# Silu in one activation, merged exponentials, and weight sums read back from DRAM, in a fused attention and gated-MLP kernel

## The chip, the cores and the metric

One core of a Trainium2 chip. The metric is the device time of the kernel in microseconds, the median of several runs; one further execution was profiled.

## What is computed

A windowed attention (window 32 in plain heads, 32 steps of 4 tokens in dilated heads), whose output feeds a gated MLP:

```python
scores = np.where(masks, q @ k.T / sqrt(64), -1e9)      # 8 batches, 8 heads, 576 tokens, head size 64
attn = exp(scores - max); attn = attn / (sum(attn) + 1e-9)
x = (attn @ v) as [4608 tokens, 512]
g = x @ w_gate                                          # 512 -> 1536
silu = g * (1.0 / (1.0 + np.exp(-g)))
return (silu * (x @ w_val)) @ w_out                     # 1536 -> 512
```

## The kernel before

The 4608 tokens are worked in six chunks. All MLP products run as float32r matmuls on operands that are split in a high and a low part, three products for each exact one.

The first three chunks have 512 tokens each. Each has 12 steps of 128 hidden features (`for s in range(NS)`). A step is 12 gate matmuls into `bank_g`, 12 value matmuls into `bank_v` (both L587) and the 12 output matmuls of the step before into `bank_o` (L636). ScalarE takes tanh(g/2) from `bank_g` (`act_tanh`, L608), DVE makes (tanh + 1) * g from it and the bank (`dve_u`, L613), then times 0.5 and the value bank (`dve_h`, L618); ScalarE and POOL split the result in two parts (`h_hi` L623, `h_lo` L628).

The last three chunks (`for ci in range(NC)`) have 1024 tokens each and multiply in blocks: sums of quarter matrices go through seven products instead of eight. A chunk has a gate stage, 6 pairs of features x 7 products x 2 matrices of 6 matmuls each (`gate_val`, L934), and an output stage of 7 x 6 x 2 groups of 3 matmuls (`outs`, L934). `keep` (L939) copies the two first banks out on ScalarE after some products, `total` adds a bank and a kept copy on DVE (L895), and `gated` makes the hidden value: tanh on ScalarE (L960), two instructions on DVE (L962, L963).

During the first chunk the weights arrive as 64-bit floats, in 24 half rows, and are turned to float32 pairs in five steps: `w_exp` (a Prelu on ScalarE), `w_shift`, `w_bits` (DVE, L280 or L283), `w_split_hi` (ScalarE), `w_split_lo` (POOL, L294). `w_load` (L243) asks for the next half row on SP's queue when a raw buffer is free.

During the second and third chunk `mix_stage` prepares the sums of weights that the seven products need, 18 steps of three stages: `mix_parts` (DVE, L801) adds the high and low parts of the kept weights, `mix_sums` (DVE L807 to L812, ScalarE L810 and L814) makes the sums, `mix_low` (DVE, L823) their low parts; `plain_parts` (L779) and `mix_out` (L831) store them to DRAM on SP's queue. POOL's queue reads them back in the last chunks (`ask`).

The attention runs in 36 packs beside all this. A pack is visited twice: an "A" visit does the scores on TensorE, `norm` of the pack before and `shift` on DVE, the exponentials on ScalarE (`far_exps`, L492 and L487) and four small exchanges of the two results on SP's queue (L497); a "B" visit the transposes. The packs 4 to 35 go through `far_exps`, 4 to 8 of them in the first chunk; none falls into the last chunk. Slots for the visits are written out in `visits`; the order on each engine is the framework's, with `behind` and `issue_after` as constraints.

Of the kernel before, what the change touches and what calls it, by code (L numbers as in the profile page):

```python
# [10 lines left out]
F32 = mybir.dt.float32  # L11
# [5 lines left out]
ALU = mybir.AluOpType  # L17

P = 128
# [21 lines left out]

NPLAIN = 3
CS = 512
NT = 7
# [2 lines left out]
KEPT = {0: 0, 2: 1, 4: 0}  # L49
SUMS = {1: ((0, 0), 1, 0), 4: ((1, 1), 2, 0), 5: ((1, 0), 1, 0), 6: ((0, 1), 2, 1)}  # L50

SEQ = [(0, 2, 1, 3, 4, 5, 6)] + [tuple(range(NT))] * (NP - 1)
PIECE = 1024
NPG = NT * NP
# [87 lines left out]
def attention_moe(ctx, tc, qkb, vb, w, masks, ident, out):  # L142
# [24 lines left out]


    pieces = tc.dram_tile([NPIECE, P, PIECE], F32, name="pieces")

    def at(o, n, dt=F32):

# [103 lines left out]
    def w_bits(u, a=0, b=3):  # L276
        y = wst[u]["y"][:, a:b]
        lo, hi = [x[:, a:b] for x in w_parts(u)]
        if by_act(u):
            nc.vector.scalar_tensor_tensor(out=y, in0=hi, scalar=3, in1=lo,  # L280
                                           op0=ALU.logical_shift_left, op1=ALU.bitwise_or)
        else:
            nc.vector.scalar_tensor_tensor(out=y, in0=lo, scalar=29, in1=y,  # L283
                                           op0=ALU.logical_shift_right, op1=ALU.bitwise_or)

    def w_place(u):
        return [wt[u][:, a:a + WU].rearrange("p (a b) -> p a b", a=3) for a in (0, WU)]

# [29 lines left out]
    def w_one(c):  # L318
        u = done[c]
        done[c] += 1  # L320
        if c == "E":
            w_exp(u)
        elif c == "T":
            w_shift(u)
        elif c == "B":
            w_bits(u)
            while ready["w"] and w_load():
                pass
        elif c == "H":
            w_split_hi(u)  # L330
        else:
            w_split_lo(u)
# [9 lines left out]
    FN = FQN  # L342
    o = M_ATT
    early, later = {}, {}
    for k, n in (("qk", QKB), ("v", NG * NH * (D + 1)), ("e", TP), ("pt", TP)):
        later[k] = Ring(n, o)
        o += n
    later["y"] = Ring(TP, M_CONST)
# [95 lines left out]
    def scores(m, two, masked):  # L444
# [9 lines left out]
        for j in range(NH):  # L454
            for g in range(NG):
                q, k = BQ * (NH * g + j), FQN + pk(m).kcol[g, j] + o
                for h in range(2):
# [2 lines left out]
                                     lhsT=t[r, q:q + BQ], rhs=t[r, k:k + w], start=not masked,  # L460
                                     stop=not masked or j == NH - 1, skip_group_check=True)

    def shift(m, two, pool, masked):

        mx, s, e = pool["bm"](2 * NH), pool["pt"](TP), pool["e"](TP)
        w = BK - 1 + masked
        a = 512 - BK - w * (NH - 1)
        x = two[:, :, a:]
        x = bass.AP(x.tensor, x.offset, [*x.ap[:2], [w, NH], [1, BK]])
        sx, ex = [t.rearrange("q (h j k) -> q h j k", h=2, j=NH) for t in (s, e)]  # L470
        if masked:
            nc.vector.tensor_copy(out=sx, in_=x)
        else:
            n, o = pk(m).far
            f = far_sb[:, BK * n:BK * n + BK]
            f = bass.AP(f.tensor, f.offset, [f.ap[0], [BK * (o - n), 2], [0, NH], [1, BK]])
            nc.vector.tensor_tensor(out=sx, in0=x, in1=f, op=ALU.add)
        n = 2 * NH
        nc.vector.reduce_max(out=mx, in_=s.rearrange("q (x k) -> q x k", x=n), axis=mybir.AxisListType.X)
        last["s"] = nc.vector.tensor_tensor(out=e.rearrange("q (c x k) -> q c x k", c=2, x=n),  # L480
                                            in0=s.rearrange("q (x c k) -> q c x k", x=n, c=2),
                                            in1=mx.unsqueeze(1).unsqueeze(3).broadcast_to([P, 2, n, BQ]), op=ALU.subtract)
        st[m]["e"], st[m]["s"] = e, s

    def exps(m):
        e = st[m]["e"]
        last["e"] = nc.scalar.activation(out=e, in_=e, func=AF.Exp, scale=0.125)  # L487

    def far_exps(m):

        e, s = st[m]["e"], st[m]["s"]
        nc.scalar.activation(out=s, in_=e, func=AF.Exp, scale=0.125)  # L492
        exps(m)
        for g in range(0, NG, 2):
            for to in range(2):
                by = 1 - to
                nc.sync.dma_start(out=e[BQ * (g + to):BQ * (g + to) + BQ, TP // 2 * by:TP // 2 * by + TP // 2],  # L497
                                  in_=s[BQ * (g + by):BQ * (g + by) + BQ, TP // 2 * to:TP // 2 * to + TP // 2])
# [104 lines left out]
    t_ring = Ring(CH, M_H, M_H + CH)  # L603
    hh_ring = Ring(CH, M_H + 2 * CH)

    def act_tanh(i):
        t = t_ring()
        last["t"] = nc.scalar.activation(out=t, in_=bank_g[:, :CH], func=AF.Tanh, scale=0.5)  # L608
        hst[i] = [t, None, None]

    def dve_u(i):
        t = hst[i][0]
        last["h"] = nc.vector.scalar_tensor_tensor(out=t, in0=t, scalar=1.0, in1=bank_g[:, :CH],  # L613
                                                   op0=ALU.add, op1=ALU.mult)

    def dve_h(i):
        t = hst[i][0]
        last["h"] = nc.vector.scalar_tensor_tensor(out=t, in0=t, scalar=0.5, in1=bank_v[:, :CH],  # L618
                                                   op0=ALU.mult, op1=ALU.mult)

    def h_hi(i):
# [169 lines left out]
    def mix_parts(n):  # L791
        i, which = divmod(n, 3)
        q = q_at.rearrange("p (f h c) -> p f h c", f=2, h=2)
        for f in range(2):
# [3 lines left out]
            for v, third in ([(u, slice(0, 3, 2))], [(u, slice(1, 2)), (u + 1, slice(0, 1))], [(u + 1, slice(1, 3))])[which]:  # L798
# [2 lines left out]
                nc.vector.tensor_tensor(out=q[:, f, h:h + k], in0=hi, in1=lo, op=ALU.add)  # L801
                h += k

    def mix_sums(n):

        a11, a12, a21, a22 = halves(n)
        nc.vector.tensor_tensor(out=a22, in0=a21, in1=a22, op=ALU.add)  # L807
        nc.vector.tensor_tensor(out=a21, in0=a11, in1=a21, op=ALU.subtract)
        with behind("e"):
            nc.scalar.copy(out=row(l_at[:, :, 0], n, 1), in_=row(q_at.rearrange("p (n c) -> p n c", n=4), n, 1))  # L810
        nc.vector.tensor_tensor(out=a11, in0=a22, in1=a11, op=ALU.subtract)
        nc.vector.tensor_tensor(out=a12, in0=a12, in1=a11, op=ALU.subtract)  # L812
        with behind("e"):
            nc.scalar.copy(out=row(l_at[:, :, 0], n, 0), in_=row(q_at.rearrange("p (n c) -> p n c", n=4), n, 0))  # L814
# [21 lines left out]
    def mix_stage():  # L836
        nonlocal mixed
        n, stage = divmod(mixed, 3)
        mixed += 1
        if n < 3 * NP:  # L840

            with behind("h", "x", "s"):
                (mix_parts, mix_sums, mix_low)[stage](n)
            with tc.issue_after(last["w"].ins):
                if stage == 0:
                    plain_parts(*divmod(n, 3))
                elif stage == 2:
                    mix_out(n)


# [103 lines left out]
    def gated(i, t):  # L954
        if t not in SUMS:
            return
        a, b = SUMS[t][0]
        g = total(t, 0, g_ring)
        f = f_ring()
        nc.scalar.activation(out=f, in_=g, func=AF.Tanh, scale=0.5)  # L960
        v = total(t, 1, v_ring)
        nc.vector.scalar_tensor_tensor(out=f, in0=f, scalar=1.0, in1=g, op0=ALU.add, op1=ALU.mult)  # L962
        nc.vector.scalar_tensor_tensor(out=hq[a, b, i], in0=f, scalar=0.5, in1=v, op0=ALU.mult, op1=ALU.mult)  # L963
        if t == 6:
            tt(nc.gpsimd, h1[i], hq[0, 1, i], hq[0, 0, i])
            tt(nc.gpsimd, hq[0, 1, i], hq[1, 1, i], hq[0, 1, i])
# [25 lines left out]
    for s in range(NS):  # L992
        ci, f = divmod(s, NF)
        W = 2 * s
        w_upto(L=W + 3, H=W + 4 - (s == 0))
        if s == 0:
            gv_first()
        else:
            gv_mm(ci, f, 0)
        act_tanh(s)  # L1000
        attend(3 * s)
        dve_u(s)
        late = visit.get(3 * s + 1, "B")[0] == "A"
        if not late:
            mix_to(2 * (s - NF) + 1)
        with behind("h", "t", "x"):
            if s == 0:
                w_upto(T=4, B=4, H=4)
                dve_h(0)
                w_part("B", 1, 1)  # L1010
                h_hi(0)
                w_part("H", 1, 1)
                w_upto(L=4)
                w_part("L", 1, 1)
                h_lo(0)
            w_upto(E=W + 6, T=W + 5, B=W + 5)
        w_upto(L=W + 4, H=W + 5)
        if s > 0:
            gv_mm(ci, f, 1)
        attend(3 * s + 1)  # L1020
        if late:
            mix_to(2 * (s - NF) + 1)
        if s > 0:
            dve_h(s)
        with behind("h", "t", "x"):
            w_upto(E=W + 7, T=W + 6, B=W + 6)
        if s > 0:
            with behind(*[("g", 0)] * (s == 1)):
                out_mm(s - 1)
            h_hi(s)  # L1030
            h_lo(s)
        if s > 0 and f == 0:
            out_store(ci - 1)
        attend(3 * s + 2)

        mix_to(2 * (s - NF) + 2)
        if ci == NPLAIN - 1:
            if f >= 9:
                with behind("l"):
                    ask([3, 5, NAT - 1][f - 9])  # L1040
            for n in {8: (0,), 9: (1, 2), 10: (3, 4, 5), 11: (6, 7)}.get(f, ()):
                x_step(n)
# [100 lines left out]
```

## Time and profile before

| | |
|---|---|
| median of 3 runs | 892.75 us (892.52 to 893.32) |
| profiled execution | 890.97 us, span 889.2 us |
| TensorE matmul busy | 879.5 us (99%) |
| DVE busy | 675.8 us (76%) |
| ScalarE busy | 380.4 us (43%) |
| POOL busy | 272.3 us (31%) |
| DMA | 207.91 MB, mean 234 GB/s |
| granted clock of TensorE | 1.00 |

The span runs from the first to the last instruction of the profiled execution, the time also holds what lies around it. Busy times of the engines overlap; "idle" is the time of an engine without an instruction, and what ended it stands behind the arrow.

### The profile page before, as it was taken

The page shows a single profiled execution, that of the slowest core. Times are in us where ns is not written, and L with a number is a line of the kernel's source. Part 1 is how long each engine was busy: PE and PEld are TensorE (multiplying, and loading weights), DVE is VectorE, ACT ScalarE, POOL GpSimd, SP SyncE. Part 2 cuts the span into 40 slices and gives each one's busy share as a digit, 9 for nine tenths or more (in the row PEclk, how much of TensorE's full clock was granted, in tenths as well). Part 3 has the DMA queues.
Part 4 walks back from the last instruction along what each step waited for, and adds up shares of the span by engine and source line. Part 5 has one row for each costly group of instructions (what it writes and reads, how often), then busy time and mean ns, then how long its engine had stood idle before and what let it go on. Part 6 is the DMA issues. An engine that isn't in the chain of part 4 may idle for free.

```text
span 889.2 us, 19625 instructions
## 1 busy us (share of the span) xinstructions
PE 879.5 (99%) x7954; PEld 719.1 (81%) x7954; DVE 675.8 (76%) x1067; ACT 380.4 (43%) x615; POOL 272.3 (31%) x313
## 2 busy tenths in 40 slices
PE   8999999999999999999999999999999999999998
PEld 5778888888888888888888888888888888888886
DVE  7876658997899993777699966787799755556963
ACT  6877533433332342333355533343455423334451
POOL 4967631211121222323333112333322113333310
PEclk9999999999999999999999999999999999999999
DMA  9975518768778775887777877887766776666672
GB/s 343 379 287 203 165 59 296 258 224 273 240 267 277 251 247 199 260 242 239 247 234 235 261 249 252 259 251 240 231 217 217 244 224 190 189 192 195 196 221 97
DMA packets 78698, 207.91 MB, mean 234 GB/s; under 512 B 9456, under 2 KB 28016, under 8 KB 78608
## 3 DMA queue, kind: packets, MB, share of 16 engines
q0 software_dynamic: 27520, 100.16, 36.8%
q1 hardware_dynamic: 41872, 70.33, 22.6%
q10 hardware_dynamic: 9216, 36.17, 11.7%
q8 instruction: 63, 1.03, 0.5%
q14 instruction: 27, 0.22, 0.1%
HBM read 159.96 MB, written 42.47 MB: 228 GB/s over the span
## 4 chain that ended last, share of the span: by engine, by line
PE 96%; DMA 2%; DVE 1%; ACT 0%; issue 0%; DVEq 0%; SPq 0%
PE bo L934 33%; PE bv L934 12%; PE bg L934 12%; PE bo L636 11%; PE bg L587 11%; PE bv L587 11%; PE two L522 3%; PE two L459 2%; DMA at_float<-qkb 1%; DMA at_int<-w 1%; ACT at_int L253 0%; DVE at_int L283 0%; DVE at_int L280 0%; DVE at_int L273 0%; ACT at_int L270 0%
## 5 line engine op out<-in xcount | busy, mean ns | idle before, releaser
L934 PE MATMUL bo<-at_float32r 128*128 128x512 f32 x1296 | 306.1, 390 | 0.0
L934 PEld LDWEIGHTS bo<-at_float32r 128*128 128x128 f32 x1296 | 242.5, 188 | 50.9
L861 POOL DMA_DIRECT2D at_float32r<-pieces x189 | 101.3, 536 | 351.0 <-PE bo L934 210.8
L895 DVE TENSOR_TENSOR at_float<-bo,at_float 128x512 f32<-128x512 f32 (+1 forms) x169 | 112.4, 679 | 66.7 <-PE bo L934 33.4
L895 DVE TENSOR_TENSOR at_float32r<-at_float,at_float32r 128x512 fp32r<-128x512 f32 (+1 forms) x147 | 112.2, 792 | 26.1 <-ACT at_float32r L924 19.5
L934 PE MATMUL bv<-at_float32r 128*128 128x512 f32 x486 | 128.2, 390 | 0.0
L934 PE MATMUL bg<-at_float32r 128*128 128x512 f32 x486 | 128.2, 390 | 0.0
L934 PEld LDWEIGHTS bg<-at_float32r 128*128 128x128 f32 x486 | 91.1, 188 | 19.0
L934 PEld LDWEIGHTS bv<-at_float32r 128*128 128x128 f32 x486 | 90.9, 188 | 19.1
L628 POOL TENSOR_TENSOR at_float32r<-at_float,at_float32r 128x512 fp32r<-128x512 f32 x36 | 51.5, 1431 | 172.8 <-PE bo L636 87.6
L636 PE MATMUL bo<-at_float32r,at_float32r 128*128 128x512 f32 x432 | 104.4, 390 | 0.0
L587 PE MATMUL bg<-at_float32r,at_float32r 128*128 128x512 f32 x420 | 101.9, 391 | 0.8 <-DVE at_float L613 0.8
L924 ACT CAST at_float32r<-at_float 128x512 fp32r<-128x512 f32 x126 | 75.4, 620 | 63.5 <-PE bv L934 16.3
L587 PE MATMUL bv<-at_float32r,at_float32r 128*128 128x512 f32 x420 | 101.7, 391 | 0.0
L636 PEld LDWEIGHTS bo<-at_float32r,at_float32r 128*128 128x128 f32 x432 | 80.7, 188 | 17.0
L587 PEld LDWEIGHTS bg<-at_float32r,at_float32r 128*128 128x128 f32 x420 | 78.3, 188 | 17.8 <-DVE at_float L613 1.2
L587 PEld LDWEIGHTS bv<-at_float32r,at_float32r 128*128 128x128 f32 x420 | 78.4, 188 | 16.6
L960 ACT ACTIVATE at_float<-at_float 128x512 f32<-128x512 f32 x72 | 45.4, 631 | 94.2 <-DVE at_float L895 94.2
L939 ACT COPY at_float<-bg 128x512 f32<-128x512 f32 x63 | 36.9, 586 | 87.8 <-PE bg L934 87.5
L895 POOL TENSOR_TENSOR at_float<-at_float,at_float 128x512 f32<-128x512 f32 x36 | 51.6, 1434 | 23.2 <-DVE at_float L963 13.0
L962 DVE SCALAR_TENSOR_TENSOR at_float<-at_float,at_float 128x512 f32<-128x512 f32 x72 | 49.4, 686 | 10.7 <-ACT at_float L960 10.1
L294 POOL TENSOR_TENSOR at_float32r<-at_int,at_float32r 128x768 fp32r<-128x768 f32 (+2 forms) x26 | 47.1, 1823 | 20.5 <-ACT at_float32r L290 20.5
(84 smaller groups left out, 856.3 us busy)
## 6 DMA issues: line engine op xcount, KB each, us to landing
at_float32r<-pieces POOLq DMA_DIRECT2D x189, 512.0 KB, 4.4
pieces<-at_float32r SPq DMA_DIRECT2D x126, 256.0 KB, 3.2
at_int<-w SPq DMA_DIRECT2D x24, 768.0 KB, 6.7
at_float<-vb ACTq DMA_DIRECT2D x31, 520.0 KB, 5.1
at_float<-qkb ACTq DMA_DIRECT2D x16, 640.0 KB, 6.6
out<-at_float SPq DMA_DIRECT2D x35, 256.0 KB, 4.0
at_float<-qkb ACTq DMA_DIRECT2D x15, 576.0 KB, 6.4
at_float<-at_float SPq DMA_DIRECT2D x128, 32.0 KB, 3.4
```

The costliest lines, as they stand in the source:

```text
L294: nc.gpsimd.tensor_tensor(out=lo, in0=wst[u]["y"][:, a:b].bitcast(F32), in1=hi, op=ALU.subtract)
L522: nc.tensor.matmul(out=two[BQ * j:BQ * j + BQ, p, (D + 1) * x:(D + 1) * (x + 1)], lhsT=t[r, BQ * i:BQ * i + BQ], rhs=v[r, i, :], start=Tru ...
L587: last["g", which] = nc.tensor.matmul(out=bank.rearrange("p (n c) -> p n c", n=2), lhsT=wcol(f, o, low), rhs=x[l][j], start=n == 0, stop=n ...
L628: last["l"] = nc.gpsimd.tensor_tensor(out=hl, in0=hst[i][0], in1=hst[i][1], op=ALU.subtract)
L636: nc.tensor.matmul(out=bank_o[j][:, :CH], lhsT=wcol(f, 2 * DM + P * j, low), rhs=x, start=f == 0 and low == 0 and x is hh, stop=f == NF - ...
L861: nc.gpsimd.dma_start(out=taken[asked], in_=pieces[asked % NPIECE])
L895: x = engine.tensor_tensor(out=out, in0=a, in1=b, op=op)
L924: nc.scalar.copy(out=o[:, 0], in_=src)
L934: nc.tensor.matmul(out=bank, lhsT=w, rhs=x, start=first and n == 0 and t in FRESH, stop=last and n == len(ops) - 1, skip_group_check=True)
L939: nc.scalar.copy(out=kept[KEPT[t]][r], in_=banks[0][r][:, :CS])
L960: nc.scalar.activation(out=f, in_=g, func=AF.Tanh, scale=0.5)
L962: nc.vector.scalar_tensor_tensor(out=f, in0=f, scalar=1.0, in1=g, op0=ALU.add, op1=ALU.mult)
```

## The change

From the second chunk on (`NTANH = 12` steps) the gate's x * sigmoid(x) comes from ScalarE's Silu in one activation; `dve_u` and one of the two DVE instructions of `gated` are left out. The two exponentials of a visit, same input, two outputs, become one instruction that reads its input twice, for which `e` and `pt` change places so that they lie side by side. Of the last three pairs of weights `w_store` writes the whole float32 weights to DRAM while the first chunk runs, and `mix_load` reads them back where `mix_parts` summed them on DVE.

```diff
+NTANH = 12
+NSUM = 3
+    whole = tc.dram_tile([NF, P, 6, UT], F32, name="whole")
+    def w_store(u):
+        a = 3 * (u % 2)
+        if u >= 4 * NSUM:
+            last["w"] = nc.sync.dma_start(out=whole[u // 2, :, a:a + 3], in_=wst[u]["y"].bitcast(F32))
             w_bits(u)
+            w_store(u)
             while ready["w"] and w_load():
-    for k, n in (("qk", QKB), ("v", NG * NH * (D + 1)), ("e", TP), ("pt", TP)):
+    for k, n in (("qk", QKB), ("v", NG * NH * (D + 1)), ("pt", TP), ("e", TP)):
+    def pair():
+        return at(later["pt"].starts[0], 2 * TP).rearrange("q (n c) -> q n c", n=2)
-        mx, s, e = pool["bm"](2 * NH), pool["pt"](TP), pool["e"](TP)
+        mx = pool["bm"](2 * NH)
+        s, e = [pair()[:, n] for n in range(2)]
-        nc.scalar.activation(out=s, in_=e, func=AF.Exp, scale=0.125)
-        exps(m)
+        last["e"] = nc.scalar.activation(out=pair(), in_=e.unsqueeze(1).broadcast_to([P, 2, TP]), func=AF.Exp, scale=0.125)
-    def act_tanh(i):
+    def act_gate(i):
         t = t_ring()
-        last["t"] = nc.scalar.activation(out=t, in_=bank_g[:, :CH], func=AF.Tanh, scale=0.5)
+        if i < NTANH:
+            last["t"] = nc.scalar.activation(out=t, in_=bank_g[:, :CH], func=AF.Tanh, scale=0.5)
+        else:
+            last["t"] = nc.scalar.activation(out=t, in_=bank_g[:, :CH], func=AF.Silu)
     def dve_u(i):
-        last["h"] = nc.vector.scalar_tensor_tensor(...)
+        if i < NTANH:
+            last["h"] = nc.vector.scalar_tensor_tensor(...)
     def dve_h(i):
-        ... scalar=0.5, in1=bank_v[:, :CH], ...
+        ... scalar=0.5 if i < NTANH else 1.0, in1=bank_v[:, :CH], ...
+    def mix_load(n):
+        i, which = divmod(n, 3)
+        thirds = (slice(0, 4, 2), slice(1, 5, 2), slice(4, 6))[which]
+        for f in range(2):
+            last["w"] = nc.sync.dma_start(out=q_at.rearrange("p (f h c) -> p f h c", f=2, h=2)[:, f], in_=whole[2 * i + f, :, thirds])
     # mix_stage
-            with behind("h", "x", "s"):
-                (mix_parts, mix_sums, mix_low)[stage](n)
+            if stage > 0 or n < 3 * NSUM:
+                with behind("h", "x", "s"):
+                    (mix_parts, mix_sums, mix_low)[stage](n)
             with tc.issue_after(last["w"].ins):
                 if stage == 0:
                     plain_parts(*divmod(n, 3))
                 elif stage == 2:
+                    if 3 * NSUM <= n + 1 < 3 * NP:
+                        mix_load(n + 1)
                     mix_out(n)
     # gated
-        nc.scalar.activation(out=f, in_=g, func=AF.Tanh, scale=0.5)
+        nc.scalar.activation(out=f, in_=g, func=AF.Silu)
         v = total(t, 1, v_ring)
-        nc.vector.scalar_tensor_tensor(out=f, in0=f, scalar=1.0, in1=g, op0=ALU.add, op1=ALU.mult)
-        nc.vector.scalar_tensor_tensor(out=hq[a, b, i], in0=f, scalar=0.5, in1=v, op0=ALU.mult, op1=ALU.mult)
+        nc.vector.tensor_tensor(out=hq[a, b, i], in0=f, in1=v, op=ALU.mult)
-        act_tanh(s)
+        act_gate(s)
```

## Rows read from the trace of the kernel before

**Rows 1.** Page, busy us (share of the span) x instructions of each engine.
```profile
PE 879.5 (99%) x7954; PEld 719.1 (81%) x7954; DVE 675.8 (76%) x1067; ACT 380.4 (43%) x615; POOL 272.3 (31%) x313
```
**Rows 2.** Chain that ended last, in order of time: start us, us, what.
```profile
29.62 3.02 PE bg L587 x12
...
119.46 2.72 PE bg L587 x12
...
869.18 16.33 PE bo L934 x72
```
**Rows 3.** Windows: us, busy PE, PEld, DVE, ACT, POOL, PEclk, DMA share, GB/s.
```profile
137.00:218.00 81.00, 81.00 (x927) 66.43 (x908) 73.32 (x126) 28.59 (x48) 17.30 (x14) 1.00 0.77 260
...
715.00:886.00 171.00, 170.50 (x753) 140.84 (x751) 103.36 (x159) 63.92 (x108) 45.77 (x69) 1.00 0.60 189
```
**Rows 4.** Waits of PE, 30 to 886 us: us in total, times, longest.
```profile
PE bg L587 <- DVE at_float L613: 0.8, 1, 0.8
```
**Rows 5.** Groups of ACT by line and form: busy us, mean ns, idle before.
```profile
L492 ACT ACTIVATE at_float<-at_float 128x512 f32<-128x512 f32 x32 | 20.2, 632 | 43.7 <-DVE at_float L480 43.6
...
L608 ACT ACTIVATE at_float<-bg 128x512 f32<-128x512 f32 x36 | 21.4, 594 | 33.4 <-PE bg L587 33.3
...
L900 ACT CAST at_float32r<-at_float 128x1024 fp32r<-128x1024 f32 x21 | 22.1, 1052 | 24.6 <-PE bo L934 13.6 <-DVE at_float L895 8.0 <-DVE at_float L555 2.5
```
**Rows 6.** Groups of DVE by line and form.
```profile
L962 DVE SCALAR_TENSOR_TENSOR at_float<-at_float,at_float 128x512 f32<-128x512 f32 x72 | 49.4, 686 | 10.7 <-ACT at_float L960 10.1
...
L613 DVE SCALAR_TENSOR_TENSOR at_float<-at_float,bg 128x512 f32<-128x512 f32 x36 | 24.5, 681 | 32.3 <-ACT at_float L608 32.3
...
L801 DVE TENSOR_TENSOR at_float<-at_float32r 128x512 f32<-128x512 f32 x24 | 17.9, 773 | 0.1
```
**Rows 7.** Timeline of ACT, first 12 us: start us, us, instruction.
```profile
1.18 1.28 ACT L678 ACT_TABLE_LOAD   x1 [1.18 <-PEq L1135]
2.48 0.20 ACT L678 ACTIVATE at_float<-at_float 128x2 f32<-128x2 f32 x1
```
**Rows 8.** Timeline of ACT, 172 to 190 us.
```profile
172.17 0.63 ACT L492 ACTIVATE at_float<-at_float 128x512 f32<-128x512 f32 x1 [3.94 <-DVE at_float L480]
...
178.92 0.59 ACT L608 ACTIVATE at_float<-bg 128x512 f32<-128x512 f32 x1
```
**Rows 9.** Timeline of PE, 176 to 182 us.
```profile
181.32 1.07 PE L587 MATMUL bg<-at_float32r,at_float32r 128*128 128x512 f32 x4
```
**Rows 10.** Timeline of ACT, 449 to 463 us.
```profile
453.00 0.63 ACT L492 ACTIVATE at_float<-at_float 128x512 f32<-128x512 f32 x1
...
458.24 0.63 ACT L960 ACTIVATE at_float<-at_float 128x512 f32<-128x512 f32 x1 [1.61 <-DVE at_float L895]
...
460.29 0.59 ACT L939 COPY at_float<-bv 128x512 f32<-128x512 f32 x1
```
**Rows 11.** Timeline of PE, 460 to 465 us.
```profile
463.00 1.52 PE L934 MATMUL bv<-at_float32r 128*128 128x512 f32 x6
```
**Rows 12.** Timeline of DVE, 310 to 322 us.
```profile
311.68 0.65 DVE L823 TENSOR_TENSOR at_float32r<-at_float,at_float32r 128x512 fp32r<-128x512 f32 x1
...
313.56 0.42 DVE L807 TENSOR_TENSOR at_float<-at_float 128x256 f32<-128x256 f32 x1
...
315.28 0.68 DVE L618 SCALAR_TENSOR_TENSOR at_float<-at_float,bv 128x512 f32<-128x512 f32 x1
```
**Rows 13.** Timeline of PE, 314 to 322 us.
```profile
321.25 1.07 PE L587 MATMUL bv<-at_float32r,at_float32r 128*128 128x512 f32 x4
```
**Rows 14.** Line L779 (`plain_parts`): issue ns min/median/max, and landing times.
```profile
L779 SPq DMA_DIRECT2D pieces<-at_float32r x54: 359/573/1464, 91.5 to 313.7; - x54
...
DMA to landing us min/median/max: 2.6/3.8/10.4
```
**Rows 15.** DMA issues: queue, count, KB each, median us to landing.
```profile
at_int<-w SPq DMA_DIRECT2D x24, 768.0 KB, 6.7
```
**Rows 16.** Timeline of POOL, 94 to 114 us.
```profile
112.67 1.75 POOL L294 TENSOR_TENSOR at_float32r<-at_int,at_float32r 128x768 fp32r<-128x768 f32 x1
```

More of the change, by code (lines that the diff above doesn't have):

```diff
@@ L612, in dve_u @@
         t = hst[i][0]
-        last["h"] = nc.vector.scalar_tensor_tensor(out=t, in0=t, scalar=1.0, in1=bank_g[:, :CH],
-                                                   op0=ALU.add, op1=ALU.mult)
+        if i < NTANH:
+            last["h"] = nc.vector.scalar_tensor_tensor(out=t, in0=t, scalar=1.0, in1=bank_g[:, :CH],
+                                                       op0=ALU.add, op1=ALU.mult)
     def dve_h(i):
         t = hst[i][0]
-        last["h"] = nc.vector.scalar_tensor_tensor(out=t, in0=t, scalar=0.5, in1=bank_v[:, :CH],
+        last["h"] = nc.vector.scalar_tensor_tensor(out=t, in0=t, scalar=0.5 if i < NTANH else 1.0, in1=bank_v[:, :CH],
                                                    op0=ALU.mult, op1=ALU.mult)
```

## Prediction

> **What bounds the kernel now.** I read the page first, for the shares of the engines: TensorE is busy 879.5 us of a span of 889.2 [rows 1]. A busy TensorE is not yet a saturated one, so the chain of waits came next, in order of time [rows 2]. The reader should see that it is TensorE alone from 29.62 us, where the second step's gate matmuls begin, to the last 72 matmuls, which end at 869.18 + 16.33 = 885.51. The pace is 2.72 us for 12, 0.2267 each, in the projection chunks, and 16.33 / 72 = 0.2268 at the end. Then the windows by stage [rows 3]: between 137 and 218 us, where DVE works 73.32 us of 81.00, TensorE is busy all 81.00; between 715 and 886, where DVE has 103.36 of 171.00, it is busy 170.50, and the missing half microsecond is the end after 885.51. So TensorE's pace doesn't follow how loaded DVE is. Last the waits of TensorE from 30 to 886 us: the largest is one of 0.8 us [rows 4], for the first chunk's `dve_u`, which this change keeps.
>
> What can be won is therefore that one wait (untouched), the 29.62 us of start, in which the change alters nothing but addresses, and the tail after 885.51, untouched too. What can be lost is found by asking how long each PSUM bank may be held before TensorE wants it back. So the views after these were the timelines of ScalarE, DVE and TensorE around the visits.
>
> **The change part by part.**
>
> *Silu for tanh.* DVE loses the 72 instructions of 686 ns at L962 (49.4 us) and 24 of the 36 of 681 ns at L613 (16.3 us) [rows 6]. ScalarE's count of activations stays; one on 128x512 costs 594 ns from PSUM as tanh and 632 ns from SBUF as exp [rows 5], and I take silu at the same. For TensorE: 0, as it doesn't wait for DVE. In the projection chunks the gate bank is now free when the activation ends, without the 0.68 us of `dve_u` behind it.
>
> *Function tables.* The trace has one table load, 1.28 us at 1.18, and the first exp starts at 2.48, 0.02 us after it ends [rows 7]; exp, tanh and the first chunk's Prelu all ran on that one. Whether silu is in the same table no row shows. Bounds: no further load, or one at every change between silu and exp. The visits of packs 4 to 8 come before the first silu, so 32 - 5 = 27 visits' exponentials have silus around them, two loads each; with the one before the first silu 55, and 55 x 1.283 = 70.6 us of ScalarE. I take 55, the dearer bound, so that a result of 0 holds for both. ScalarE then has about 380 + 71 - 7 = 444 us of work, half the span, so only the places matter.
>
> In a projection chunk the tightest is the visit at 172.17 [rows 8]. Its exp waits 3.94 us for DVE, which hides the load before it. The later activation stands at 178.92 right behind a cast, so its load is exposed: 178.92 + 1.28 + 0.59 = 180.79, with 0.1 us for lost overlap 180.89. TensorE overwrites the gate bank at 181.32 [rows 9]. 0.43 us are left: cost 0.
>
> In a gate stage the tightest is the visit at 453.00 [rows 10]. The exp there waited for nothing, so the load's 1.28, less 0.20 for the merged exponentials (below), delays the queue by 1.08. The activation at 458.24 waited 1.61 us, which hides the second load. The copy of the second bank ends at 461.96 instead of 460.29 + 0.59 = 460.88; TensorE wants that bank at 463.00 [rows 11]. 1.04 left. I went through the other 25 visits in the same way and none is below 0.43. Cost: 0.
>
> The Trainium skill, "ScalarE: Activation LUTs", section "What ACT_TABLE_LOAD costs", adds a drain of about 1.38 us to a load of 1.283, 2.66 us a switch; the trace agrees on the 1.283 and shows no drain, but its one load had no work in front. By the page's price the sum would be some +7 us, by the row 0. The page's section "Table sets" names exp and tanh in one set and doesn't name silu there, which speaks for the 55.
>
> *A visit's exponentials in one.* Two of 0.632 become one of 128x1024; the nearest row is the cast of that shape, 1.052 [rows 5]. 2 x 0.632 - 1.052 = 0.21 less a visit, 32 x 0.21 = 6.8 us of ScalarE; if there were no saving, the spares above shrink by 0.2 and stay positive. On the path 0: the four transfers behind it needed both already. The exchanged places of `e` and `pt` move addresses only: 0.
>
> *Weights through DRAM.* `w_store` adds 12 DMAs of 0.39 MB on SP, each behind its `w_bits`, for which the next weight load waits anyway, and ahead of that load. The loads land later by something between 0 and the 6.7 us that twice the size takes [rows 15]. What waits for them: the last part of the last half row is ready at 112.67 + 1.75 = 114.42 [rows 16], and the chunk's last step begins at 119.46 [rows 2], its value matmuls, which are the first to read that half row, 2.72 later. 7.8 us of cover against at most 6.7: cost 0. Without the cover it would be the slip.
>
> `mix_load` replaces `mix_parts` for 9 of 18 steps. DVE loses half of L801, whose larger form takes 17.9 us [rows 6]: 9 us and something for the smaller form. SP gains 18 DMAs, issued when `mix_low` of the step before has freed the buffer, ahead of its four stores, the next three, and any visit's exchanges queued behind them: 18 x 0.57 = 10 us of issue [rows 14]. DVE's sums now wait for a transfer. Nearest row: the 256 KB stores of L779, 2.6 / 3.8 / 10.4 us from issue to landing [rows 14]. Tightest is the last step: `mix_low` before it ends at 311.68 + 0.65 = 312.33, the sums stood at 313.56 [rows 12]. With 0.57 for the second issue and 3.8 they start at 316.7, 3.1 later than now. Behind them on DVE stands `dve_h` (L618, 315.28), which would end about 3.2 later, at 319.2; TensorE wants the value bank at 321.25 [rows 13]. 2.1 left: cost 0. At the slowest landing, 10.4, it ends at 325.8, 4.5 late. Bounds 0 and 4.5 for such a step; I take 0, as the median is 2.1 away from the edge.
>
> Sum: 0, with up to 0.3 for small stalls where 0.43 is thin. The profiled execution took 890.97, its span of 889.2 and 1.8 around it; the median of the runs is 1.8 above it. The span becomes 889.2 to 889.5; as a median 892.75 + 0.15 = 892.9.
>
> **The rivals.**
>
> *A load costs twice its row when work stands around it*, 2.57 instead of 1.28 us. For it: the only load shown stands at an idle engine. Against it: 0.02 us from load to exp. Then the activation at 178.92 ends 0.9 late; at the gate visit the delay is 2.57 - 0.20 + 2.57 - 1.61 = 3.33, the copy 1.2 late, or 1.6 with the overlaps that loads break up. Over the 27 visits four come out 0.5 to 1.6 late (4.6 in all) and six about 0.1: +5, 898. It decides from about 1.7 a load on. The Trainium skill's 2.66, named above, is this rival and a little more.
>
> *Loads from DRAM come late.* For it: DVE reaches the sums as early as 1.2 us after `mix_low`, and 10.4 has been seen. Against: DVE has 75 us less to do and the median leaves 2.1. One or two late ones, up to 4.5 each, give +2 to +8, about 897. It decides from a landing of 5.9 us.
>
> *Faster: TensorE is held up by DVE and ScalarE inside its busy time.* For it: weight loads are busy only 719.1 us [rows 1]. Against: the pitch is 0.227 in loaded and light stages alike. If 75 us less on DVE took 0.3% off the pitch, 855.9 x 0.003 = 2.6 us go: 890. It decides from 0.2% on. The Trainium skill, "Perfetto Trace Analysis", section "Identifying the Most-Contended Engine", calls matmul busy time a bad measure and takes the weight loads' share; by that, 81% here, room would be left, which the even pitch contradicts.
>
> *Silu shares exp's table*: no loads, same time; it is inside the forecast.
>
> **How the numbers follow.** A change of 0.2%, 1.8 us, is about what a measurement of this kernel can tell. Forecast 0.74 (by itself 891.3 to 894.3), dear loads 0.10, late transfers 0.12, faster 0.04. So faster 0.04, same 0.74, slower 0.22. From 891.1 to 898 leaves out the faster case, half of the dear loads and the worst of the late transfers, under 2 in 10.
>
> **What would show it.** Right: TensorE busy 879 to 880; DVE near 600; about 55 table loads and ScalarE near 444; no L962; one activation a visit near 1.05; waits of DVE at L807 for `whole`. Wrong: TensorE waiting in a gate or value matmul for ScalarE behind a table load, a gap around each load, or L618 ending late after 220 us. A second step that begins later than 29.6 would mean that the order at the front moved.

## The result and the profile after

The changed kernel takes 902.28 us (900.18 to 902.91, 4 runs) against 892.63 for the kernel before on the same chip: ratio 1.0103, 95% interval 1.0085 to 1.0121. It is slower by 9.65 us, where no change was forecast. The profiled execution took 902.91 us, span 901.1.

The page of the changed kernel: busy us of each engine (share of the span) and instructions, which answers to [rows 1].

```profile
PE 884.1 (98%) x7954; PEld 720.4 (80%) x7954; DVE 609.6 (68%) x947; ACT 441.9 (49%) x636; POOL 271.3 (30%) x313
```

DVE has lost 66 us, where 75 were forecast, and ScalarE gained 61.5 of 64; the span has grown by 11.9 all the same. Some 1.7 us of that belong to the profiled execution of before, which was a short one: it took 890.97, the four timed beside the result 892.15 to 893.32.

The windows by stage (columns as in [rows 3]) show where. First one of the kernel before, then those of the changed kernel:

```profile
220.00:312.00 92.00, 91.99 (x1011) 75.57 (x1010) 84.92 (x144) 32.74 (x54) 14.42 (x11) 1.00 0.77 262
```
```profile
137.00:220.00 83.00, 83.00 (x1033) 68.05 (x1021) 69.56 (x121) 40.63 (x54) 18.80 (x14) 1.00 0.75 248
220.00:312.00 92.00, 85.07 (x971) 68.64 (x969) 60.00 (x102) 40.49 (x52) 12.73 (x9) 0.98 0.85 280
...
343.00:530.00 187.00, 186.62 (x1788) 153.03 (x1787) 131.85 (x207) 95.66 (x140) 51.52 (x75) 1.00 0.78 241
```

From 137 to 220 us silu, table loads and merged exponentials run already, and TensorE is busy all 83.00. Between 220 and 312 it misses 92.00 - 85.07 = 6.93 us, where it was busy 91.99 before, and the granted clock averages 0.98. The first read from `whole` is issued at 223.95. The gate stage after it misses 0.38.

The waits of TensorE from 30 to 898 us (columns as in [rows 4]):

```profile
PE two L534 <- DVE at_float L523: 3.8, 2, 3.0
PE bv L599 <- DVE at_float L634: 1.7, 1, 1.7
PE bg L599 <- ACT at_float L623: 1.1, 1, 1.1
PE bg L599 <- DVE at_float L629: 0.8, 1, 0.8
PE bo L960 <- DVE at_float L921: 0.6, 2, 0.4
PE bo L652 <- ACT at_float32r L639: 0.4, 1, 0.4
```

Only the 0.8 was there before. The 0.6 (L921) lies in the gate stages. The other new ones end on four different instructions: the transposed exponentials (L523), `dve_h` (L634), the silu (L623), `h_hi` (L639). That is the sign of a common cause further back. The same question put to DVE and to SP's queue of the changed kernel:

```profile
DVE at_float L830 <- DMA at_float<-whole: 21.9, 7, 5.3
```
```profile
SPq L795 <- DMA at_float<-whole: 8.2, 4, 4.4
```

DVE's first sum of a step (L830, formerly L807) waited 21.9 us in seven of the nine steps for its read. Four times the plain stores (L795, formerly L779) waited for a read to land: the program gives its transfers eight semaphores in turn, so that each waits for the one eight places ahead of it, and the reads take places.

One of the waits followed through, from the timelines of the changed kernel. DVE, 237 to 247 us:

```profile
237.31 0.69 DVE L493 TENSOR_TENSOR at_float<-at_float,at_float 128x512 f32<-128x512 f32 x1
241.83 0.42 DVE L830 TENSOR_TENSOR at_float<-at_float 128x256 f32<-128x256 f32 x1 [3.83 <-DMA at_float<-whole]
...
243.10 0.40 DVE L831 TENSOR_TENSOR at_float<-at_float 128x256 f32<-128x256 f32 x1
```

ScalarE:

```profile
243.58 0.62 ACT L833 CAST at_float32r<-at_float 128x512 fp32r<-128x512 f32 x1 [3.65 <-DVE at_float L831]
244.46 0.62 ACT L837 CAST at_float32r<-at_float 128x512 fp32r<-128x512 f32 x1 [0.25 <-DMA pieces<-at_float32r]
245.10 1.28 ACT L623 ACT_TABLE_LOAD   x1
246.39 0.60 ACT L623 ACTIVATE at_float<-bg 128x512 f32<-128x512 f32 x1
```

TensorE:

```profile
247.04 3.02 PE L599 MATMUL bg<-at_float32r,at_float32r 128*128 128x512 f32 x12 [1.11 <-ACT at_float L623]
```

The reader is to see that the silu waits for nothing of its own: its gate values were done at 240.5. It stands in ScalarE's order behind two casts of the weight sums, these behind DVE's sums, and these behind the read.

The longest wait stands behind the sums as well. DVE, 301 to 308 us:

```profile
301.51 0.43 DVE L830 TENSOR_TENSOR at_float<-at_float 128x256 f32<-128x256 f32 x1 [5.34 <-DMA at_float<-whole]
...
306.45 0.69 DVE L846 TENSOR_TENSOR at_float32r<-at_float,at_float32r 128x512 fp32r<-128x512 f32 x1
307.05 0.70 DVE L523 STREAM_TRANSPOSE at_float<-at_float 128x512 f32<-128x512 f32 x1
```

From the read's landing on DVE works without a break, and the transpose of the exponentials (L523) comes behind the sums and their low parts in its order. It ends at 307.75, and TensorE starts again at 307.81 after 3.01 us.

SP's queue was late too, but not the last. SP's timeline:

```profile
297.21 4.70 SPq L795 DMA_DIRECT2D pieces<-at_float32r  x3
302.19 2.41 SPq L509 DMA_DIRECT2D at_float<-at_float  x4
```

The visit's exponentials ended at 295.61 + 1.06 = 296.67; their four exchanges (L509) leave behind the stores, at 302.19. They land within 3.4 us of their issue, the last at about 306.2, while DVE is still at the sums.

### The profile page after: what moved, and what is told of

It is laid out like the page before. It is cut to its first block, busy times and chain, and to the rows that moved or that the text cites. A ratio compares the mean times of both kernels' runs of the same rounds, so it can differ in the third digit from the quotient of the medians.

```text
span 901.1 us, 19633 instructions
## 1 busy us (share of the span) xinstructions
PE 884.1 (98%) x7954; PEld 720.4 (80%) x7954; DVE 609.6 (68%) x947; ACT 441.9 (49%) x636; POOL 271.3 (30%) x313
## 4 chain that ended last, share of the span: by engine, by line
PE 88%; DMA 5%; DVE 3%; ACT 1%; issue 1%; SPq 1%; POOL 0%; DVEq 0%; ACTq 0%; POOLq 0%
PE bo L960 31%; PE bg L960 12%; PE bv L960 12%; PE bg L599 9%; PE bo L652 9%; PE bv L599 9%; DMA pieces<-at_float32r 3%; PE two L534 3%; PE two L468 2%; DMA at_float<-at_float 1%; PE fs L411 1%; DMA at_float<-qkb 1%; DVE at_float32r L846 1%; DMA at_float<-whole 0%; DVE at_int L283 0%
## 5 line engine op out<-in xcount | busy, mean ns | idle before, releaser
L921 DVE TENSOR_TENSOR at_float<-bo,at_float 128x512 f32<-128x512 f32 (+1 forms) x169 | 112.7, 682 | 94.0 <-ACT at_float L965 45.7
L921 DVE TENSOR_TENSOR at_float32r<-at_float,at_float32r 128x512 fp32r<-128x512 f32 (+1 forms) x147 | 113.9, 807 | 34.9 <-ACT at_float32r L950 27.8
L988 DVE TENSOR_TENSOR at_float<-at_float,at_float 128x512 f32<-128x512 f32 x72 | 49.2, 686 | 15.9 <-ACT at_float L986 13.3
L921 POOL TENSOR_TENSOR at_float<-at_float,at_float 128x512 f32<-128x512 f32 x36 | 50.0, 1388 | 25.0 <-DVE at_float L988 22.1
```

What stands on the lines that cost most here:

```text
L921: x = engine.tensor_tensor(out=out, in0=a, in1=b, op=op)
L988: nc.vector.tensor_tensor(out=hq[a, b, i], in0=f, in1=v, op=ALU.mult)
```

## The experiments

Times of before are those of the same chip; a ratio stands with its 95% interval. Theory "transfers": the weights read back from DRAM cost the time. Theory "tables": the function-table loads do.

**No weights through DRAM.**

```diff
-NSUM = 3
+NSUM = 6
```


> The changed kernel with all 18 steps summed on DVE: no weights through DRAM (NSUM = 6), silu and merged exponentials kept. Theory 'transfers' (the stalls between 240 and 310 us come from the reads of the summed weights): these stalls of some 9 us go, 893 to 895 us. Theory 'tables' (they come from the function-table loads in front of ScalarE's silu): they stay, 900 to 902. Theory 'both are needed': they go as well, 893 to 895, and the next run tells it from the first.

893.35 us against 892.85, ratio 1.0007 (0.9998 to 1.0017). The loss is gone, silu, 53 loads and merged exponentials still there. Its waits of TensorE from 30 us on are those of the kernel before:

```profile
PE bg L599 <- DVE at_float L629: 0.8, 1, 0.8
PE two L534 <- issue: 0.3, 1, 0.3
```

"Tables" has fallen.

**DRAM alone**, on the kernel before: `whole`, `w_store`, `mix_load` and the condition in `mix_stage` added, nothing else of the change.

> The kernel before with the weights through DRAM alone (stores, reads, 9 steps not summed on DVE), tanh and two exponentials kept, so one table load. 'Transfers': 898 to 901 us, with TensorE waiting between 240 and 310. 'Tables': 892 to 893.5. 'Both are needed': 892.5 to 895.

901.81 against 892.85, 1.0094 (1.0075 to 1.0114), 0.8 above the range expected, with one table load in the whole kernel. All of the loss, so silu isn't needed for it. DVE waits here too:

```profile
DVE at_float L822 <- DMA at_float<-whole: 16.5, 8, 4.7
```

**Stores ahead of the reads.**

```diff
-                    if 3 * NSUM <= n + 1 < 3 * NP:
-                        mix_load(n + 1)
                     mix_out(n)
+                    if 3 * NSUM <= n + 1 < 3 * NP:
+                        mix_load(n + 1)
```


> The changed kernel with the four stores of a step issued before the two reads for the next one, nothing else. If the reads hurt by standing ahead of the stores (the stores land late, the next stores and the visit's exchanges stand behind them in SP's queue): 894 to 898 us, SP's long stays at the three plain stores go from 5 to 6 us to 2. If they hurt by keeping DVE's sums waiting: reads come later, so 902 to 906.

908.96, 1.0184 (1.0168 to 1.0199): 6.7 us worse than the change, more even than expected of late sums. The reads, which also leave later, now land 5.8 us after issue in the median instead of 3.4, and DVE waits in all nine steps:

```profile
DVE at_float L830 <- DMA at_float<-whole: 35.5, 9, 6.0
```

**Stores only.** Of the change, `w_store` without `mix_load`; DVE sums all 18 steps.

> The changed kernel with the 12 stores of whole weights in the first chunk but without the reads: all 18 steps summed on DVE. 'Transfers' with the reads as the cause: as the run without DRAM within 0.5 us. If the stores in the first chunk cost something (the start or the weight loads): 1 us or more above it, seen before 220 us.

894.23, 1.0018 (1.0009 to 1.0028). That is 0.9 above the run without DRAM, between the two expectations, and the intervals overlap, so that it isn't clear of noise. No wait of TensorE in its profile says where 0.9 us would be; this stays open.

**Two pairs instead of three** (NSUM = 4), the control for the next run.

> The changed kernel with the weights of the last two pairs instead of three through DRAM (NSUM = 4): reads for 6 steps, not 9. Control for the next run. If each read late by itself costs: two thirds of 9 us, 898 to 900 us. If the loss grows along the loop (each read waits for the sums of the one before): the last six hold most of it, 899 to 901.

899.48 against 893.08, 1.0068 (1.0051 to 1.0084): +6.4 for six reads of nine. It doesn't tell the two expectations apart.

**A second buffer**, so that the read leaves a step earlier.

```diff
-    q_at = at(M_RAW, PIECE)
+    q_all = [at(M_RAW, PIECE), at(M_X1 + 6 * CS, PIECE)]
+    def q_of(n):
+        return q_all[n >= 3 * NSUM and n % 2 == 0]
                 if stage == 0:
                     plain_parts(*divmod(n, 3))
+                    if 3 * NSUM <= n + 1 < 3 * NP:
+                        mix_load(n + 1)
                 elif stage == 2:
-                    if 3 * NSUM <= n + 1 < 3 * NP:
-                        mix_load(n + 1)
                     mix_out(n)
```


> As the control, but with a second buffer for the summed weights, in a place that is free by then, so that a step's two reads are issued at the first stage of the step before instead of at its end. Theory 'late sums' (DVE and, behind it, ScalarE's casts stand in order behind sums whose read left too late): TensorE's waits go, 893 to 895 us. Theory 'SP's queue' (the plain stores and the visit's exchanges stand behind the reads): little better than the control, 897 to 900.

894.70, 1.0018 (1.0008 to 1.0027): 4.8 of the control's 6.4 us are gone, with the same bytes on the same queue and a landing no quicker (median 4.4 and up to 7.9, in the control 3.5 and 8.4). DVE waits once:

```profile
DVE at_float L834 <- DMA at_float<-whole: 2.1, 1, 2.1
```

**Reads on POOL's queue.**

```diff
-            last["w"] = nc.sync.dma_start(out=q_at..., in_=whole[...])
+            nc.gpsimd.dma_start(out=q_at..., in_=whole[...])
```


> The changed kernel with the 18 reads issued on POOL's queue instead of SP's, at the same point of the program. 'SP's queue': SP is rid of them, 894 to 897 us. 'Late sums': the read still starts after the sums of the step before and lands 4 us or more later, 899 to 904.

908.71, 1.0173 (1.0158 to 1.0188). SP has no read any more and the loss grows: the reads land after 4.7 us in the median, DVE waits 24.8 + 2.8 us. That speaks against SP's queue as the main cause. It is also above the 904 expected of late sums, and the run is no clean test of the queue: POOL itself now waits 45.0 us, in nine waits, for the low parts that free the buffer before it can issue the reads, and its own work (`h_lo`) stands behind these in its order. What that adds was not measured.

**Plain stores early**: those of the last nine steps during the first nine.

```diff
-                if stage == 0:
+                if stage == 0 and n < 3 * NSUM:
                     plain_parts(*divmod(n, 3))
+                elif stage == 1 and n < 3 * NSUM:
+                    plain_parts(*divmod(n + 3 * NSUM, 3))
```


> The changed kernel with the plain stores of the last nine steps issued during the first nine, so that SP has only reads, four stores a step and the visits' exchanges when the reads run. 'SP's queue': the exchanges leave at once, the waits for the transposes at 268 and 308 us go (4 us and the clock's share of 1), 895 to 898. 'Late sums': 899 to 902, TensorE's waits for the gate and value banks stay.

901.88, 1.0094 (1.0068 to 1.0119), no better than the change. In its profiled execution, a short one of 898.26, the wait for the transposes is 1.1 instead of 3.8 us, while the gate bank's (1.6), the value bank's (0.7) and DVE's for the reads (20.5) stay. The exchanges left early there, at 296.13, but this isn't what made the wait shorter. Its DVE and, after the wait, its TensorE:

```profile
298.15 0.43 DVE L830 TENSOR_TENSOR at_float<-at_float 128x256 f32<-128x256 f32 x1 [3.79 <-DMA at_float<-whole]
```
```profile
304.45 0.81 PE L534 MATMUL two<-at_float,at_float 64*32 64x65 f32 x60 [1.09 <-DVE at_float L523]
```

From the first sum to TensorE's start are 304.45 - 298.15 = 6.30 us, and in the changed kernel 307.81 - 301.51 = 6.30 too. The read came earlier, and all behind it on DVE took the same. No wait of TensorE is shown to come from SP's queue by itself.

**Reads that nobody waits for.** As the control, but the reads go to a buffer of their own and DVE sums all 18 steps.

```diff
+    q_none = at(M_X1 + 6 * CS, PIECE)
-... nc.sync.dma_start(out=q_at..., in_=whole[...])
+... nc.sync.dma_start(out=q_none..., in_=whole[...])
-            if stage > 0 or n < 3 * NSUM:
+            if True:
```


> The control with two pairs through DRAM, but its reads go to a buffer that nothing reads, and DVE sums all 18 steps as in the kernel before: the same 12 transfers stand at the same places of SP's queue, and no sum waits for them (the output is complete). 'Late sums': 893 to 894.5 us, like the run without DRAM. 'Traffic or SP's queue': 897 to 900, like the control.

893.40 against 891.74, 1.0017 (1.0008 to 1.0027), where the control has 1.0068. The reads land no sooner after their issue (median 5.2, up to 8.6), but nobody minds: the traffic and the places in SP's queue without the dependence cost about what the stores alone do. The places are the same in the program's order, not in time: as the reads needn't wait for the buffer either, they leave from 250.2 to 302.7 us, in the control from 258.2 to 316.5.

**Few bytes for the packs.** The runs up to here leave open why some reads land after 7 to 8 us and most after 3 to 4. In the changed kernel's profile three of the nine steps have their read issued next to the loads of a pack. Its ScalarE queue, 215 to 345 us (L377 values, L371 queries and keys, together about 1.1 MB):

```profile
234.20 0.33 ACTq L377 DMA_DIRECT2D at_float<-vb  x1
...
269.69 0.33 ACTq L377 DMA_DIRECT2D at_float<-vb  x1
270.32 1.29 ACTq L371 DMA_DIRECT2D at_float<-qkb  x1
291.16 0.33 ACTq L377 DMA_DIRECT2D at_float<-vb  x1
293.37 0.34 ACTq L371 DMA_DIRECT2D at_float<-qkb  x1
```

The reads beside them are issued at 234.83, 270.46 and 292.52. So these three visits' loads were cut to a few columns:

```diff
+                few = m in (15, 17, 18)
                 if m > 4:
-                    load_v(m, later, nc.scalar)
+                    load_v(m, later, nc.scalar, few)
                 if m + 1 < NPK:
-                    load_qk(m + 1, later, nc.scalar)
+                    load_qk(m + 1, later, nc.scalar, few)
```


> The change, but the loads of values and queries that three visits issue at the time of a read (at 234, 270 and 291 us in the changed kernel's profile) fetch 8 columns and one group instead of 1.1 MB; the attention of those packs is computed on what an earlier pack left in the buffer. In the profile of the change the reads issued with such a load land after 6 to 9 us and the others after 3 to 4, and the three longest waits of DVE for a read (3.8, 5.2, 5.3 us) stand there. Theory that the coincidence makes these reads late and that the late ones cost the time: all nine steps wait at most 2.5 us for their read, the waits of TensorE of 1.1, 1.7 and 3.0 us go, and the time is 893 to 896. Rival, that the loop of sums, release and read is too long at the ordinary landing of 3 to 4 us: the time stays at 899 to 902.

892.61 against 891.47, ratio 1.0011 (1.0002 to 1.0020), slightly better than expected: the loss is gone but for about what the stores cost. All other work is there, the loads from DRAM too. The landing times of its reads (L828):

```profile
DMA to landing us min/median/max: 2.7/3.2/4.5
```

In the changed kernel they are 2.6, 3.4 and 8.3. The median is nearly the same; the slow ones are missing. DVE still waits in seven steps, 9.9 us and 3.0 at most (2.5 were expected), and TensorE waits once, 1.4. So the ordinary landing costs a little too.

**Few bytes elsewhere**, the control: the same for m in (14, 16, 19).

> The same for three visits whose loads are issued away from a read (at 219, 254 and 309 us), as the control: as many bytes fewer, and the attention of those packs on what an earlier pack left. Theory of the coincidence: no gain or a small one, 900 to 902. Were the amount of traffic between 219 and 312 us what counts, it would gain as much as the other run, 893 to 896.

900.88 against 891.47, 1.0111 (1.0097 to 1.0125): as slow as the change. Not the amount of traffic counts, but which read it meets: DVE's longest waits for a read are 3.9, 4.3 and 3.8 us, in the same three steps. Its waits of TensorE from 30 us on begin with these:

```profile
PE two L536 <- DVE at_float L525: 2.0, 1, 2.0
PE bg L601 <- ACT at_float L625: 1.7, 1, 1.7
```

**Loads doubled**, on the run without DRAM.

```diff
+        if m >= 9:
+            nc.scalar.activation(out=some, in_=e[:, :2], func=AF.Gelu)
         last["e"] = nc.scalar.activation(out=pair(), ..., func=AF.Exp, scale=0.125)
+        if m >= 9:
+            with behind("e"):
+                nc.scalar.activation(out=some, in_=some, func=AF.Gelu)
```


> The changed kernel without DRAM (NSUM = 6), with a small Gelu on two columns before and after each exponential of the visits from pack 9 on, so that every switch between exp and silu takes two table loads and one activation of 0.2 us instead of one load: some 108 loads. By the working of the prediction a switch of 2.6 to 2.8 us makes TensorE wait at about ten of the 27 visits, 5 to 8 us in all: 898 to 901. If the loads lie in ScalarE's idle time whatever they cost: 893 to 894.5.

901.06 against 891.74, 1.0103 (1.0086 to 1.0120): +9.3, with 111 loads of 1283 ns besides the one at the start and 54 small Gelus. Its waits of TensorE from 30 us on:

```profile
PE bo L965 <- DVE at_float L926: 1.9, 4, 0.7
PE bg L604 <- ACT at_float L628: 1.7, 1, 1.7
PE two L539 <- issue: 1.4, 2, 1.1
```

So the loads do have a price, at twice their number, and the first two kinds of waits stand where the working had looked for them, at a bank of the gate stages and at the gate bank behind the silu. Its sum was 1.3 to 4.3 us short.

## Why the prediction was wrong

*What bounds the kernel*: right. TensorE is saturated, the pitch at the end is still 16.33 us for 72. The rival "faster" fell: the run without DRAM has less work on DVE (625.0 us against 675.8) and is no faster. The sign "a second step that begins later than 29.6" came, 29.99, but says little: it is 29.86 without DRAM and 29.41 with the stores alone.

*Silu, tables, exponentials*: right, 0 forecast, 0.5 us measured, with an interval that includes no change. The table loads are 26, 14, 13 and the first, 54 where 55 were forecast. ScalarE's groups of the changed kernel (columns as in [rows 5]):

```profile
L505 ACT ACTIVATE at_float<-at_float 128x1024 f32<-128x1024 f32 x32 | 34.0, 1062 | 18.5 <-DVE at_float L493 14.1 <-DMA at_float<-qkb 3.9
L505 ACT ACT_TABLE_LOAD x26 | 33.4, 1283 | 5.9 <-issue 3.1 <-DMA pieces<-at_float32r 1.5 <-PE two L468 0.9
L986 ACT ACT_TABLE_LOAD x14 | 18.0, 1283 | 3.5 <-DVE at_float L921 3.2
L623 ACT ACT_TABLE_LOAD x13 | 16.7, 1283 | 0.2
```

1283 ns each, the price of [rows 7], and 1.062 for the merged exponentials, forecast 1.05. The rival "a load costs twice its row" fell by the timeline of ScalarE at a load with work right in front of it:

```profile
222.53 0.60 ACT L623 ACTIVATE at_float<-bg 128x512 f32<-128x512 f32 x1 [4.64 <-PE bg L599]
223.15 1.28 ACT L505 ACT_TABLE_LOAD   x1
224.44 1.06 ACT L505 ACTIVATE at_float<-at_float 128x1024 f32<-128x1024 f32 x1
```

From the silu's end at 223.13 to the exp at 224.44 are 1.31 us. The Trainium skill, "ScalarE: Activation LUTs", section "What ACT_TABLE_LOAD costs", has 2.66 with a drain; the measurement decides here for 1.31. That the price mattered is shown by the doubled loads.

*`w_store`*: 0 forecast, about 0.9 measured, hardly clear of noise and not located.

*`mix_load`*: this is the step that failed. It said of the last step, taken as the tightest: "2.1 left: cost 0", and took 0 "as the median is 2.1 away from the edge". The median landing was sized well, 3.4 us against 3.8 [rows 14]. What was wrong is what hangs on it, in three ways.

First, the wrong step was taken for the tightest. The last step was chosen for its room on DVE, but its read is issued at 319.11, 9 us before the next load of a pack, and its sums start 3.9 later. What decides is which reads meet a pack's loads, and for two of the three this could be seen before the change. DVE's low parts (`mix_low`, whose end releases the buffer) of the kernel before:

```profile
267.11 0.69 DVE L823 TENSOR_TENSOR at_float32r<-at_float,at_float32r 128x512 fp32r<-128x512 f32 x1
...
283.72 1.46 DVE L823 TENSOR_TENSOR at_float32r<-at_float,at_float32r 128x512 fp32r<-128x512 f32 x2
```

and its ScalarE queue:

```profile
266.63 0.35 ACTq L368 DMA_DIRECT2D at_float<-vb  x1
267.25 0.70 ACTq L362 DMA_DIRECT2D at_float<-qkb  x1
284.59 0.34 ACTq L368 DMA_DIRECT2D at_float<-vb  x1
```

The buffer comes free at 267.80 and 285.18, within 1.2 us of a load's issue. The third late read could not be told in this way: the buffer is free at 231.13 and the load leaves at 233.45, while at 298.32 and 299.90 the two are nearer and the read of that step was not late after the change. Windows of the changed kernel over a read with and one without such loads:

```profile
270.50:279.30 8.80, 8.17 (x36) 6.39 (x35) 3.48 (x8) 2.56 (x3) 0.00 (x0) 1.00 0.95 287
284.00:288.00 4.00, 4.00 (x19) 3.23 (x18) 1.30 (x3) 2.21 (x3) 1.87 (x2) 1.00 0.73 226
```

The DMA engines are 95% busy in the one and 73% in the other. The working had read the slow landings of [rows 14] as bad luck that any transfer may meet. For the reads they come at the same places: these three steps have DVE's longest waits in the profiles of the DRAM-alone run, the plain-early run and the second control too.

Second, the spare was measured at one consumer, `dve_h`. It was late once (the 1.7 at 280.37). Behind the sums stand also ScalarE's two casts, with the silu and its table load behind them (1.1 at 247.04), and DVE's transpose of the exponentials (3.0 at 307.81). These were never asked how much they had. The three waits, with 0.4 at 283.74 behind the second, are 6.2 of the 6.9 us between 220 and 312; the other 0.7, at 268.80, stands behind an ordinary read. The 0.4 has a second source: the cast in front of it waited until 282.03, 1.4 us longer than for its sum, for stores of earlier sums (`mix_out`, L854) that were issued right behind the late read and landed after 8.3 to 8.7 us.

Third, a wait was counted by its length alone. Towards the end of TensorE's 3.01 us of waiting the granted clock falls to 0.50 and stays there for a while. Windows of the changed kernel, behind the wait and after:

```profile
307.50:310.90 3.40, 3.09 (x131) 2.73 (x132) 1.77 (x5) 0.69 (x2) 1.27 (x1) 0.50 0.97 319
311.00:330.00 19.00, 19.00 (x207) 15.57 (x206) 11.15 (x23) 8.24 (x11) 2.38 (x3) 1.00 0.87 279
```

By the chain the visit and the 12 matmuls at 307.81 take 1.19 + 0.87 + 3.43 = 5.49 us, those at 233.37 take 0.72 + 0.03 + 0.03 + 0.62 + 3.00 = 4.40: 1.1 us more.

The sum as the profile gives it: 6.9 of waits between 220 and 312, 1.1 by the clock, 0.6 of waits in the gate stages, whose source was not followed: 8.6. The profiled execution lies 902.91 - 892.63 = 10.28 above the median before. Of the other 1.7 the stores may be 0.9, by the difference of two runs; the rest is open.

The rival "loads from DRAM come late" was right in mechanism, and its edge of 5.9 us fits: reads of 7 us and more cost time, one of 5.8 (issued at 307.16) nothing, reads of 3 to 4 little, 0.7 here and 1.4 in the run with few bytes. Its chance, 0.12, and its size, one or two late ones and 897 us, were wrong, because the late landing was taken for chance. It is a matter of the schedule: the same three steps in four profiles.

The other runs fit. A second buffer gives the read a step more, so that a landing of 7.9 us is still in time. Behind the stores, or on POOL's queue, the reads land 2.4 and 1.3 us later in the median, and steps become late that had been in time.

No version here is faster than the kernel before: with TensorE saturated, the best of them equal it.

## What to carry to other kernels

Before work is put behind a new transfer, look in the trace at what the other queues issue within a few us of the place where it will leave, and take the landing for each place by itself: a median, and the place with the least room on the engines, both miss it. Then follow everything that is queued behind the instruction that will wait, on its engine and the next ones, and take the least spare of all. Where some places are late, try a second buffer and an earlier issue before another queue: here the first won back 4.8 of 6.4 us, and the second made it worse.

## What the runs showed of the hardware

The granted clock of TensorE fell from 1.00 to 0.50, of the two levels 2.4 and 1.2 GHz the lower, towards the end of its wait of 3.01 us, and the next matmuls ran at that; after the waits of 1.11 and 1.71 us of the same execution the profile shows no fall. The length of the wait alone doesn't settle it: in other profiles the clock also fell right after waits of 1.84 us (DRAM alone, at 248) and 2.03 us (the second control, at 307), and not after one of 2.73 (two pairs, at 305). Where it falls, a wait costs more than its own length: 1.1 us on top of 3.0 here.

A table load is 1283 ns whichever function it is for (exp, silu, and Gelu in the doubled run), and 0.01 to 0.02 us stand between it and its neighbours even with work in front. Silu took a load behind exp, and exp behind silu, at all 53 changes.

Of the 18 reads of 256 KB in the changed kernel's profile, four, issued beside about 1.1 MB of another queue's loads, landed after 7.0 to 8.3 us, and the others after 2.6 to 5.8. With the bytes beside them taken away none took more than 4.5; as many bytes taken away elsewhere in the same 90 us gained nothing.
